# Another scheme of seven block products in a planned attention and feed-forward kernel

## The chip, the cores and the metric

The kernel runs on one core of a Trainium2 chip. The metric is the device time of one execution in microseconds; before the change the median of three runs is 946.24 us (943.14 to 946.65). The profile is of one more execution, which took 943.59 us, with 941.8 us from its first to its last instruction.

In the profile PE is TensorE (matmuls), PEld its loads of the stationary operand, DVE is VectorE, ACT is ScalarE, POOL is GpSimd, and SP issues DMAs. L441 is line 441 of the kernel. The clock column is the share of full speed that TensorE was granted.

## The reference

Two parts follow each other, all in float32:

```python
scores = scale * np.matmul(q, k.transpose(0, 1, 3, 2))        # 8 x 8 heads, 576 positions, 64 wide
mask = (rel >= 0) & (rel < 64)                                # each position sees itself and 63 before it
attn = softmax of the masked scores
attn_out = np.matmul(attn, v)
x = attn_out, tokens by heads                                 # 4608 x 512
h = x @ w_in                                                  # 512 x 2048
g = np.where(h >= 1, h, np.where(h <= -1, 0.0, (h + 1) ** 2 / 4.0))
out = g @ w_out                                               # 2048 x 512
```

## The kernel before, in words

**Tiles.** The 4608 tokens are nine tiles of 512. For each tile four attention steps `s` (128 tokens each, all heads) make the columns of x, and then the feed-forward part makes 16 blocks of 128 features from them and adds each block's share to four accumulators (L902).

**Two-part numbers.** Each operand of the feed-forward matmuls is split in a high part (rounded to TensorE's float32r) and a low part (the rest), and three matmuls stand for one: high-high, high-low, low-high. ACT or DVE rounds (copy and cast, L256 and L258), DVE or POOL subtracts (L527 for x, L885 for g, L716 for weights).

**An attention step.** Scores (L397) go to two PSUM banks, one for each half of the heads. From step 8 on, for each half apart: DVE scales and masks them into a tile `sm` (L409), finds the negative maximum (L413), ACT takes exponents and their sums (L420), DVE adds a small number and inverts (L427, L428), DVE or POOL normalises (L432), and DVE transposes 32-row pieces into a tile `ptd` (L441), 12 for each half. There are four tiles `sm` and three `ptd`. Then TensorE multiplies with v (L461). The result goes to a tile `u`.

**Seven products.** The first two tiles compute h plainly (L851). From the third tile on (`PLAIN = 2`), two feature blocks, two halves of the input features and two halves of the tile's tokens are a 2 x 2 by 2 x 2 block product that is done with seven products in place of eight (L786). The x side of the seven operands is made in a "build", one for each half of the columns of the tile: sums and differences of blocks (L511, L515), then the high and low parts `xs`. The weight side is made once, while the second tile runs (`sum_...`, L693, L704, L716), kept in HBM (`kept`) and loaded again for each tile in two rings (`wr`, tags `ra` and `rb`). A pair of feature blocks is computed by 24 matmuls (four products into two banks a and b, each of two halves of 256 columns), four dependent steps that empty these banks (L256 or L258, L802), then 18 matmuls (three products that add to what stands in the banks). The blocks of h stand in SBUF: the tile `h` has four blocks of 256 columns, two for each feature block. Before the change the first four products give two differences or sums of bank halves, the next three complete the two middle blocks in bank a (one copy of 512 columns), and SBUF blocks are added to each other (L806, L817, L818).

**The gate.** For each feature block: relu on ACT (L863), square (L868), min and max with h on DVE (L875), the high part `gh` on ACT (L880), the low part `gl` on POOL (L885), then 12 matmuls (L902). There are two buffers each of `a`, `gh` and `gl`.

**What sets the order.** The program adds items to a plan (`add`): a key (the place in the sequence at which the item is wanted), costs in ns for each engine that could do it, what it waits for, and which buffers it takes and gives back. `Plan.run` chooses again and again the item that can start first, within a patience the one of smallest key, puts it on its cheapest engine, and so writes each engine's instruction list. On the chip an engine works off its list in that order and waits where an operand is not ready.

Of the kernel before, what the change touches and what calls it, by code (L numbers as in the profile page):

```python
# [20 lines left out]
P = 128  # L21
# [61 lines left out]
BUFS = dict(qt=2, kt=2, vt=4, ps_a=2, sm=4, ptd=3, x=2, u=2, ps_h=2, a=2, gh=2, gl=2, acc=4, o=2, h=2, ra=2, rb=2, tmp=2)  # L83
# [5 lines left out]
B_KEY = 4 / 3  # L89
O_AFTER = 14 / 3  # L90
O_BEFORE = 0
EARLY_2 = 1.5
N_SPLIT = 8
# [6 lines left out]
A_EARLY = 1.5  # L100
# [85 lines left out]
def banded_attention_then_ffn(ctx: ExitStack, tc: tile.TileContext, q, k, v, w, masks, out, dims):  # L186
# [13 lines left out]
    att = ctx.enter_context(tc.tile_pool(name="att", bufs=BUFS["sm"]))  # L200
# [37 lines left out]
    ptd = [const.tile([P, NP, SB], F32, name=f"ptd{i}") for i in range(BUFS["ptd"])]  # L238
# [118 lines left out]

    def variant(s):
# [26 lines left out]
    def att_scores(s, masked, pool):  # L385
# [7 lines left out]
        for p in range(NP):  # L393
            for i in range(SB // m):
                r = slice(i * m, (i + 1) * m)
                for h in range(2):
# [3 lines left out]
                    )  # L400
        for h in range(2):
            blk[s, h] = banks[h][:, :, :n], att.tile([P, NP, WIN], F32, name="sm")[:, :, :n], *(
                att.tile([P, NP], F32, name=n) for n in ("nm", "den"))
# [30 lines left out]
    def att_transpose(s, h, i, js):  # L434


        sm, pt = blk[s, h][1], ptd[(2 * seq[s] + h) % len(ptd)]
        for j in js:
# [10 lines left out]
    def att_transposed(s, h, eng):  # L449
        copy(eng, ptd[(2 * seq[s] + h) % len(ptd)], pts.pop((s, h)))  # L450

    def att_values(s, pool):

        vt, pt = [vts.pop((s, i)) for i in range(2)], [ptd[(2 * seq[s] + h) % len(ptd)] for h in range(2)]
# [30 lines left out]
    def x_tiles(t):  # L485
# [9 lines left out]
        xops[t] = a, b, rest, [a[:, 0], rest[0], a[:, 1], b[:, 1], rest[1], rest[2], b[:, 0]]  # L495

    xtmp = {}

    def x_source(t, r, k):
        x = [xfs[t, r][:, j].rearrange("p (c e) n -> p e c n", e=2) for j in range(2)]  # L500
        if k == 0:
            return xtmp[t, r][:, :2]
        return (x[1], x[0][:, 0], x[1][:, 1], xtmp[t, r][:, 2])[k - 1]

    def x_sums(t, r, eng):
        xtmp[t, r] = d = ffn.tile([P, 4, 2, SB], F32, name="u", bufs=BUFS["u"])
        x = [xfs[t, r][:, j].rearrange("p (c e) n -> p e c n", e=2) for j in range(2)]
        for i, (a, b, op) in enumerate((
            (x[1][:, 0], x[1][:, 1], ALU.subtract), (x[0][:, 0], x[1][:, 1], ALU.add), (x[0][:, 1], x[0][:, 0], ALU.subtract)
        )):  # L510
# [600 lines left out]
```

## Time and profile before

| | |
|---|---|
| median of three runs | 946.24 us (943.14 to 946.65) |
| the profiled execution | 943.59 us, span 941.8 us |
| TensorE busy | 889.8 us, 94%, granted clock 0.979 |
| VectorE busy | 762.1 us, 81% |
| ScalarE busy | 523.7 us, 56% |
| GpSimd busy | 377.6 us, 40% |
| HBM | 162.15 MB read, 24.12 MB written, 198 GB/s over the span |

The shares are averages over stages: up to about 25 us q, k, v and weights arrive; to 250 us the two plain tiles run, the second with the weights' sums beside it; then seven tiles in cycles of about 100 us with four attention steps for the next tile in each; the last 80 us have no attention. A cycle is read best between two equal points, and a wait by what ended it.

### The profile page before, as it was taken

The page shows a single profiled execution, that of the slowest core. Times are in us where ns is not written, and L with a number is a line of the kernel's source. Part 1 is how long each engine was busy: PE and PEld are TensorE (multiplying, and loading weights), DVE is VectorE, ACT ScalarE, POOL GpSimd, SP SyncE. Part 2 cuts the span into 40 slices and gives each one's busy share as a digit, 9 for nine tenths or more (in the row PEclk, how much of TensorE's full clock was granted, in tenths as well). Part 3 has the DMA queues.
Part 4 walks back from the last instruction along what each step waited for, and adds up shares of the span by engine and source line. Part 5 has one row for each costly group of instructions (what it writes and reads, how often), then busy time and mean ns, then how long its engine had stood idle before and what let it go on. Part 6 is the DMA issues. An engine that isn't in the chain of part 4 may idle for free.

```text
span 941.8 us, 20899 instructions
## 1 busy us (share of the span) xinstructions
PE 889.8 (94%) x7839; PEld 766.9 (81%) x7839; DVE 762.1 (81%) x1800; ACT 523.7 (56%) x1322; POOL 377.6 (40%) x392
## 2 busy tenths in 40 slices
PE   7799998989789999899989999899989998999998
PEld 5688887867578888788878888788878887898997
DVE  6999997988999947979797989798887979774342
ACT  7898855555455545454554555445635554644443
POOL 1000035786453623436343545254433634352222
PEclk8999999999899999999999999999989999999999
DMA  8991148458376558476665667566846673647531
GB/s 322 402 355 46 57 137 280 155 198 278 120 243 234 179 180 270 138 235 208 212 214 186 213 189 242 180 209 205 254 134 211 205 258 113 190 158 220 178 118 45
DMA packets 108037, 187.63 MB, mean 199 GB/s; under 512 B 8480, under 2 KB 49696, under 8 KB 107936
## 3 DMA queue, kind: packets, MB, share of 16 engines
q1 hardware_dynamic: 107648, 185.38, 59.8%
q8 instruction: 62, 1.02, 0.4%
q10 hardware_dynamic: 288, 0.92, 0.3%
q14 instruction: 39, 0.32, 0.1%
HBM read 162.15 MB, written 24.12 MB: 198 GB/s over the span
## 4 chain that ended last, share of the span: by engine, by line
PE 51%; DVE 28%; ACT 6%; DMA 6%; issue 4%; POOL 4%; SPq 0%; ACTq 0%; DVEq 0%; POOLq 0%
PE acc L902 23%; PE ps_h L786 18%; DVE ptd L441 9%; PE ps_h L851 5%; DVE a L875 5%; ACT sm L420 3%; PE ps_a L461 2%; PE ps_a L397 2%; DMA kept<-half 2%; DVE u L511 2%; DMA kt<-in_k 2%; ACT a L863 1%; DVE xs L527 1%; DMA out<-o 1%; DVE sm L409 1%
## 5 line engine op out<-in xcount | busy, mean ns | idle before, releaser
L902 PE MATMUL acc<-wts,gh 128*128 128x512 f32 x1154 | 367.7, 400 | 18.5 <-ACT gh L880 15.9
L786 PE MATMUL ps_h<-xs,wr 128*128 128x256 f32 x2352 | 305.7, 285 | 2.5 <-DVE h L802 2.0
L786 PEld LDWEIGHTS ps_h<-xs,wr 128*128 128x128 f32 x2352 | 293.4, 192 | 15.4 <-DVE h L802 5.1
L885 POOL TENSOR_TENSOR gl<-a,gh 128x512 fp32r<-128x512 f32 (+1 forms) x130 | 172.0, 1324 | 316.8 <-ACT gh L880 273.9
L902 PEld LDWEIGHTS acc<-wts,gh 128*128 128x128 f32 x1154 | 213.7, 193 | 60.4 <-ACT gh L880 17.7
L902 PE MATMUL acc<-wts,gl 128*128 128x512 f32 x577 | 230.1, 399 | 7.8 <-POOL gl L885 7.5
L441 DVE STREAM_TRANSPOSE ptd<-sm 32x128 f32<-32x128 f32 x696 | 210.1, 302 | 11.1
L880 ACT CAST gh<-a 128x512 fp32r<-128x512 f32 (+1 forms) x149 | 89.5, 602 | 151.8 <-PE acc L902 95.5
L902 PEld LDWEIGHTS acc<-wts,gl 128*128 128x128 f32 x577 | 110.6, 192 | 37.4 <-POOL gl L885 13.5
L875 DVE SCALAR_TENSOR_TENSOR a<-a,h 128x512 f32<-128x512 f32 x112 | 96.2, 859 | 30.5 <-ACT a L868 28.8
L420 ACT ACTIVATE sm<-sm,nm 128x96 f32<-128x96 f32 (+1 forms) x256 | 93.2, 366 | 44.6 <-DVE nm L413 44.6
L863 ACT ACTIVATE a<-h 128x512 f32<-128x512 f32 x112 | 70.1, 626 | 64.1 <-DVE h L813 53.1
L851 PE MATMUL ps_h<-xh,wts 128*128 128x512 f32 (+1 forms) x296 | 87.8, 365 | 3.0 <-DVE a L875 1.9
L868 ACT ACTIVATE a<-a 128x512 f32<-128x512 f32 (+1 forms) x141 | 87.0, 617 | 4.3
L256 ACT COPY h<-ps_h 128x256 f32<-128x256 f32 (+1 forms) x102 | 46.7, 465 | 67.4 <-PE ps_h L786 67.0
L813 DVE TENSOR_TENSOR h<-h,ps_h 128x256 f32<-128x256 f32 x56 | 23.4, 419 | 69.3 <-PE ps_h L786 69.1
L693 POOL TENSOR_TENSOR half<-wts 128x256 f32<-128x256 f32 x18 | 13.4, 766 | 144.0 <-PE ps_h L851 127.0
L851 PEld LDWEIGHTS ps_h<-xh,wts 128*128 128x128 f32 x296 | 53.8, 190 | 12.5 <-DVE a L875 2.1
L802 DVE TENSOR_TENSOR h<-h,ps_h 128x256 f32<-128x256 f32 x112 | 46.7, 417 | 11.1 <-ACT h L256 8.3
L851 PE MATMUL ps_h<-xl,wts 128*128 128x512 f32 (+1 forms) x148 | 53.7, 363 | 0.5 <-DVE xl L474 0.5
L461 PEld LDWEIGHTS ps_a<-ptd,vt 128*64 128x64 f32 x992 | 33.4, 140 | 18.2 <-DVE ptd L441 6.6
L420 ACT ACTIVATION_READ_ACCUMULATOR sm<-sm,nm 128x1 f32 x256 | 48.2, 188 | 0.0
(101 smaller groups left out, 968.8 us busy)
## 6 DMA issues: line engine op xcount, KB each, us to landing
wr<-kept SPq DMA_DIRECT2D x112, 512.0 KB, 4.7
wr<-kept SPq DMA_DIRECT2D x112, 384.0 KB, 3.9
vt<-in_v SPq DMA_DIRECT2D x72, 256.0 KB, 4.0
kt<-in_k SPq DMA_DIRECT2D x35, 384.0 KB, 4.2
raw<-in_w SPq DMA_DIRECT2D x12, 1023.8 KB, 11.2
qt<-in_q SPq DMA_DIRECT2D x36, 256.0 KB, 3.6
out<-o SPq DMA_DIRECT2D x32, 256.0 KB, 4.3
kept<-wts SPq DMA_DIRECT2D x32, 128.0 KB, 2.1
```

What stands on the lines that cost most here:

```text
L256: nc.scalar.copy(dst, src)
L420: nc.scalar.activation(sm[:, p, :], (ps if masked else sm)[:, p, :], AF.Exp, bias=nm[:, p:p + 1], scale=scale if masked else 1.0, accum_ou ...
L441: nc.vector.transpose(pt[(c + j) * SQ:(c + j + 1) * SQ, :, r], sm[r, :, c * SQ:(c + 1) * SQ])
L461: nc.tensor.matmul(ps[half[h], p, n], lhsT=vt[i][:, c:c + D], rhs=pt[h][:, p, n], start=True, stop=True)
L786: nc.tensor.matmul(ps[:, c * 2 * SB:(c + 1) * 2 * SB], lhsT=r[:, part, cp, o], rhs=xo[k][:, xp, cp], start=i == 0 and c == 0 and j == 0 an ...
L851: nc.tensor.matmul(ps, lhsT=wts[f, 0][:, part, c * P:(c + 1) * P], rhs=x[:, c, r], start=(c == 0 and j == 0), stop=(c == NP - 1 and j == 2),)
L863: nc.scalar.activation(gs[t, f, r.start][0], phs[t, f, r.start], AF.Relu, bias=0.5, scale=0.5)
L868: nc.scalar.activation(a, a, AF.Square)
L875: nc.vector.scalar_tensor_tensor(out=a, in0=a, scalar=1.0, in1=ps, op0=ALU.min, op1=ALU.max)
L880: nc.scalar.copy(g[1], g[0])
L885: engine[eng].tensor_tensor(out=g[2], in0=g[0], in1=g[1].bitcast(F32), op=ALU.subtract)
L902: nc.tensor.matmul(acc[t, i][:, n], lhsT=g[:, sub], rhs=wts[f, 1][:, part, n], start=(q == 0 and j == 0), stop=(q == NF - 1 and j == 2 and ...
```

## The change

**Products.** Another scheme of seven products is used. Other sums of x and of weights are made: four differences of x blocks, each an item of its own (`x_sums`, before one item of three and a total), and four sums of weight blocks (before five), with three weight blocks copied unchanged instead of two. The four blocks of h are completed by adding from banks: one copy of 256 columns and three additions after the first 24 matmuls, two additions and a copy of 256 after the 18. No SBUF block is added to another.

**Halves of heads.** From step 8 on the two halves share one tile `sm` of double width (two such tiles), and one item each finds the maxima, inverts the sums, and transposes: 12 pieces of 32 x 256, each an item. They write the first two of the three `ptd` tiles, as one buffer (`pt2`).

**Order.** Costs of some items in the plan are larger, output matmuls of the first block of a tile and of the last are items of 128 tokens, and the keys of attention (`A_EARLY`) and of the outputs at the change from plain tiles (`O_CHANGE`) are other ones.

```diff
-BUFS = dict(qt=2, kt=2, vt=4, ps_a=2, sm=4, ptd=3, x=2, ...
+BUFS = dict(qt=2, kt=2, vt=4, ps_a=2, sm=2, ptd=3, pt2=1, x=2, ...
-A_EARLY = 1.5
+A_EARLY = 5
...
+    def att_transpose_both(s, i, j, c):
+        r = slice(i * QB + j * SQ, i * QB + (j + 1) * SQ)
+        src = blk[s, BOTH][1][r].rearrange("p h a n -> p (h a) n")
+        dst = ptq[(c + j) * SQ:(c + j + 1) * SQ, :2].rearrange("p h a n -> p (h a) n")
+        nc.vector.transpose(dst[:, :, r], src[:, :, c * SQ:(c + 1) * SQ])
...
+    def x_sums(t, r, j, eng):
+        if j == 0:
+            xtmp[t, r] = ffn.tile([P, 4, 2, SB], F32, name="u", bufs=BUFS["u"])
+        d = xtmp[t, r]
+        x0, x1 = x_halves(t, r)
+        i, a, b = ((0, x1[:, 0], x0[:, 0]), (2, x1[:, 1], x1[:, 0]), (1, x1[:, 1], d[:, 0]), (3, x0[:, 1], d[:, 1]))[j]
+        engine[eng].tensor_tensor(out=d[:, i], in0=a, in1=b, op=ALU.subtract)
...
-        return dict(DVE=65 * k + 1.04 * n, Pool=200 * k + 2.1 * n)
+        return dict(DVE=100 * k + 1.5 * n, Pool=200 * k + 2.3 * n)
...
+            (6, 2, 3, ALU.add), (4, 6, 0, ALU.subtract), (5, 0, 2, ALU.subtract), (7, 1, 4, ALU.subtract)
...
-            ((a, 0, 3, 0), (a, 1, 0, 1), (b, 0, 1, 2), (b, 1, 2, 3)),
-            ((a, 0, 2, 4), (a, 1, 0, 5), (b, 0, 1, 6)),
+            ((a, 0, 0, 0), (a, 1, 1, 1), (b, 0, 2, 2), (b, 1, 3, 3)),
+            ((b, 0, 2, 5), (b, 1, 0, 6), (a, 0, 1, 4)),
...
+    def h_copy(t, n, to, eng):
+        copy(eng, h_of(t, n)[:, to:to + 256], prods[t, n][0][:, :256])
+
+    def h_add(t, n, to, of, bank_, at):
+        h, ps = h_of(t, n), prods[t, n][bank_]
+        nc.vector.tensor_tensor(out=h[:, to:to + 256], in0=h[:, of:of + 256], in1=ps[:, at:at + 256], op=ALU.add)
...
+        m = [add(key, take, lambda e: h_copy(t, n, 512, e), [xa])]
+        for v in (256, 512, 0, 256), (768, 256, 1, 0), (768, 768, 1, 256):
+            m.append(add(key, cost, lambda e, v=v: h_add(t, n, *v), m[-1:]))
         xb = add(
             key + B_KEY, dict(PE=18 * (12.5 + 256 * .4175)), lambda e: ffn_products(t, n, 1), [rb, xa, *m],
...
+        xl = add(key, cost, lambda e: h_add(t, n, 512, 256, 1, 0), [xb, m[1]])
+        xf = add(key + Y_LATE, cost, lambda e: h_add(t, n, 256, 256, 1, 256), [xl], gives=[("ps_h", xa, 1)])
+        xm = add(key + Y_LATE, take, lambda e: h_copy(t, n, 0, e), [xb], gives=[("ps_h", xa, 0)])
...
-                ends = t == len(TILES) - 1 and q == NF - 1 and r.stop == TILES[t]
-                for i0 in subs(r) if ends else [None]:
+                by_sub = t >= PLAIN and q == 0 or t >= PLAIN - 1 and q == NF - 1
+                for i0 in subs(r) if by_sub else [None]:
```

**How it moves instructions.** Three places follow, first before, then with the change. The first is VectorE where it has most to do in a cycle. Before, that is the build of the first half of a tile (three sums, L511, stand just ahead); `ptd` and `sm` are attention's tiles, `xs` the operands, `h` the blocks of features, `a` the gate's tile.

```order
L441 STREAM_TRANSPOSE ptd_119<-sm 32x4x32 x3
L258 CAST xs<-u 128x2x128
L258 COPY h<-ps_h 128x512
L527 TENSOR_TENSOR xs<-u,xs 128x2x2x128
L813 TENSOR_TENSOR h<-h,ps_h 128x256
L527 TENSOR_TENSOR xs<-u,xs 128x2x128
L427 TENSOR_SCALAR den<-den 128x4
L428 RECIPROCAL den<-den 128x4
L527 TENSOR_TENSOR xs<-u,xs 128x2x128
L432 TENSOR_TENSOR sm<-sm,den 128x4x96
L441 STREAM_TRANSPOSE ptd_119<-sm 32x4x32 x3
L875 SCALAR_TENSOR_TENSOR a<-a,h 128x512
```

With the change the pair with most rows of VectorE's work is the one in which the build of the second half begins:

```order
L828 TENSOR_TENSOR h<-h,ps_h 128x256 x2
L447 STREAM_TRANSPOSE ptd<-sm 32x8x32
L828 TENSOR_TENSOR h<-h,ps_h 128x256
L447 STREAM_TRANSPOSE ptd<-sm 32x8x32 x10
L828 TENSOR_TENSOR h<-h,ps_h 128x256
L447 STREAM_TRANSPOSE ptd<-sm 32x8x32
L828 TENSOR_TENSOR h<-h,ps_h 128x256
L884 SCALAR_TENSOR_TENSOR a<-a,h 128x512 x2
L529 TENSOR_TENSOR u<-u 128x256 x4
L259 CAST xs<-u 128x2x2x128
```

The gates (L875, now L884) stood behind the build's sums and low parts, and now stand ahead of the sums; no low part of `xs` is in these rows any more.

The second place is VectorE in the other of the two builds of a tile, before the second half's:

```order
L802 TENSOR_TENSOR h<-h,ps_h 128x256
L258 COPY h<-ps_h 128x256
L802 TENSOR_TENSOR h<-h,ps_h 128x256
L806 TENSOR_TENSOR h<-h 128x256
L511 TENSOR_TENSOR u<-u 128x256 x3
L258 CAST xs<-u 128x2x128 x2
L258 COPY h<-ps_h 128x512
L813 TENSOR_TENSOR h<-h,ps_h 128x256
```

and with the change the first half's:

```order
L828 TENSOR_TENSOR h<-h,ps_h 128x256
L259 CAST xs<-u 128x2x2x128
L828 TENSOR_TENSOR h<-h,ps_h 128x256
L259 CAST xs<-u 128x2x128 x2
L828 TENSOR_TENSOR h<-h,ps_h 128x256
L418 SCALAR_TENSOR_TENSOR sm<-ps_a,nmsk 128x384 x2
L422 TENSOR_REDUCE nm<-sm 128x8
```

The build's casts stood behind the two additions that the 18 products wait for, and now three casts stand between the three additions (L828) that they wait for.

The third place is GpSimd's list around the build of the first half, before:

```order
L885 TENSOR_TENSOR gl<-a,gh 128x512
L527 TENSOR_TENSOR xs<-u,xs 128x2x128
L515 TENSOR_TENSOR u<-u 128x512
L817 TENSOR_TENSOR h<-h 128x256
L818 TENSOR_TENSOR h<-h 128x256
L527 TENSOR_TENSOR xs<-u,xs 128x2x2x128
L885 TENSOR_TENSOR gl<-a,gh 128x512 x2
```

and with the change:

```order
L894 TENSOR_TENSOR gl<-a,gh 128x512 x2
L529 TENSOR_TENSOR u<-u 128x256 x2
L894 TENSOR_TENSOR gl<-a,gh 128x512
L541 TENSOR_TENSOR xs<-u,xs 128x2x2x128 x2
L541 TENSOR_TENSOR xs<-u,xs 128x2x128 x3
L894 TENSOR_TENSOR gl<-a,gh 128x512 x2
```

All five low parts (L541) of this build are now GpSimd's, and the additions of blocks of `h` are gone from its list.

More of the change, by code (lines that the diff above doesn't have):

```diff
@@ L356, in banded_attention_then_ffn, with pt_of @@
     half = [slice(0, D), slice(D, P)]
+    def pt_of(s, h):
+        return h if s >= SOON else (2 * seq[s] + h) % len(ptd)
     def variant(s):
@@ L644, in add_step @@
-            ready.append(x)
+                    due, dict(DVE=440), lambda e, piece=piece: att_transpose_both(s, *piece),
+                    ready if ends else taken or x, takes=["pt2"] * (not n), gives=[("sm", xs)] * ends,
+                )
+                ready.append(x)
+                first = taken = taken or [x]
+            gives = [("pt2", taken[0])]
         last["t"] = first
         needs = ready + [xv, xw]
-        gives = [("ptd", taken[0]), ("ptd", taken[1]), ("vt", xv), ("vt", xw)]
+        gives += [("vt", xv), ("vt", xw)]
```

246 lines of the change are left out of this document (117 added, 129 removed).

## The prediction

> **What bounds the kernel now.** I read the page's busy times first, then stretches of the span, then what TensorE waited for, then one such wait in the timeline.
>
> ```profile
> PE 889.8 (94%) x7839; PEld 766.9 (81%) x7839; DVE 762.1 (81%) x1800; ACT 523.7 (56%) x1322; POOL 377.6 (40%) x392
> ```
>
> TensorE is nearly always busy and its instruction counts stay the same after the change (2352 products, 1731 output matmuls, all else equal), so only its waits and its clock can be won. Where are they? The next view is busy time by stretch (start:end, length, then busy us and instruction count of PE, PEld, DVE, ACT, POOL, then granted clock, DMA share, GB/s).
>
> ```profile
> 391.57:491.13 99.56, 95.31 (x913) 83.29 (x913) 85.38 (x209) 52.09 (x137) 45.34 (x43) 1.00 0.64 207
> 491.13:590.77 99.64, 96.31 (x912) 84.37 (x912) 85.37 (x209) 51.85 (x137) 45.37 (x43) 0.98 0.64 207
> 590.77:691.76 100.99, 96.38 (x913) 84.43 (x913) 85.38 (x209) 52.08 (x137) 45.34 (x43) 0.98 0.65 207
> 691.76:792.07 100.31, 97.47 (x912) 85.16 (x912) 85.36 (x209) 52.17 (x137) 45.28 (x43) 0.97 0.62 196
> 877.22:919.30 42.08, 42.08 (x267) 38.16 (x266) 17.04 (x36) 18.05 (x33) 10.54 (x8) 1.00 0.44 140
> 165.00:250.00 85.00, 75.21 (x664) 59.17 (x662) 76.79 (x188) 44.73 (x130) 63.24 (x77) 0.99 0.59 196
> 250.00:310.00 60.00, 54.35 (x566) 46.65 (x565) 57.02 (x144) 30.58 (x91) 23.44 (x24) 0.94 0.66 221
> ```
>
> The first four are whole cycles of a tile (eight pairs of feature blocks, four attention steps), on average 100.1 us. The fifth is four pairs of the last tile, with no attention beside them: 42.08 / 4 = 10.52 us each, with no gap. What a step adds to TensorE shows between two sets of 18 products:
>
> ```profile
> 605.15 2.32 PE L786 MATMUL ps_h<-xs,wr 128*128 128x256 f32 x18
> 610.14 0.99 PE L397 MATMUL ps_a<-kt,qt 64*32 64x96 f32 x64
> 616.79 2.32 PE L786 MATMUL ps_h<-xs,wr 128*128 128x256 f32 x18
> 627.40 1.15 PE L461 MATMUL ps_a<-ptd,vt 128*64 128x64 f32 x32
> 628.48 2.42 PE L786 MATMUL ps_h<-xs,wr 128*128 128x256 f32 x18
> ```
>
> 616.79 - 605.15 = 11.64 holds one set of scores, so scores cost 1.12; 628.48 - 616.79 = 11.69 holds one set of values, so values cost 1.17. A cycle that never waited would take 8 x 10.52 + 4 x 1.12 + 4 x 1.17 = 93.3 us. The four cycles are 6.8 us above that on average.
>
> ```profile
> PE acc L902 <- ACT gh L880: 15.9, 8, 4.7
> PE acc L902 <- POOL gl L885: 7.5, 9, 1.6
> PE ps_a L461 <- DVE ptd L441: 5.8, 6, 2.1
> ```
>
> The output matmuls (L902) wait for the gated activations gh and gl. One such wait closes each cycle; the timeline shows who is late:
>
> ```profile
> 687.27 1.29 POOL L527 TENSOR_TENSOR xs<-u,xs 128x512 fp32r<-128x512 f32 x1
> 687.46 1.38 DVE L527 TENSOR_TENSOR xs<-u,xs 128x256 fp32r<-128x256 f32 x1
> 688.03 0.63 ACT L868 ACTIVATE a<-a 128x512 f32<-128x512 f32 x1
> 689.34 0.94 DVE L441 STREAM_TRANSPOSE ptd<-sm 32x128 f32<-32x128 f32 x3
> 690.30 0.69 DVE L875 SCALAR_TENSOR_TENSOR a<-a,h 128x512 f32<-128x512 f32 x1
> 691.09 0.62 ACT L880 CAST gh<-a 128x512 fp32r<-128x512 f32 x1 [2.42 <-DVE a L875]
> 691.76 1.22 PE L902 MATMUL acc<-wts,gh 128*128 128x512 f32 x2 [2.76 <-ACT gh L880]
> 693.70 1.06 PE L902 MATMUL acc<-wts,gh 128*128 128x512 f32 x2
> ```
>
> ACT's cast waited for the gate on DVE (L875), and DVE had no gap: it was busy with the next tile's operands (L527), normalising and transposing. After the wait TensorE's pair of matmuls takes 1.06, a cost that the 6.8 includes. The pair of feature blocks in which it happens:
>
> ```profile
> 675.05:695.55 20.50, 17.16 (x114) 14.16 (x113) 19.38 (x42) 10.03 (x30) 10.86 (x10) 0.89 0.54 175
> ```
>
> From its first addition L802 to the next pair's, DVE has 19.38 us of work, against 11.7 (10.52 + 1.17) of TensorE's. So TensorE sets the pace over the cycle, and DVE, 85.4 of 100, sets it in one burst per cycle. Between 165 and 310 us (the weights' sums, the first products) DVE is busy 133.8 of 145 us; TensorE idles 9.8 + 5.65 = 15.4 us there, and the granted clock takes 85 x 0.01 + 60 x 0.06 = 4.5 more.
>
> **The change part by part.** Durations come from the groups by shape (count | busy us, mean ns of one | idle before):
>
> ```profile
> L441 DVE STREAM_TRANSPOSE ptd<-sm 32x128 f32<-32x128 f32 x696 | 210.1, 302 | 11.1
> L802 DVE TENSOR_TENSOR h<-h,ps_h 128x256 f32<-128x256 f32 x112 | 46.7, 417 | 11.1 <-ACT h L256 8.3
> L806 DVE TENSOR_TENSOR h<-h 128x256 f32<-128x256 f32 x27 | 17.9, 662 | 0.9
> L817 DVE TENSOR_TENSOR h<-h 128x256 f32<-128x256 f32 x31 | 15.7, 505 | 0.0
> L818 DVE TENSOR_TENSOR h<-h 128x256 f32<-128x256 f32 x31 | 15.3, 492 | 1.1
> L258 DVE COPY h<-ps_h 128x256 f32<-128x256 f32 x56 | 23.4, 417 | 5.6 <-PE ps_h L786 5.5
> L258 DVE COPY h<-ps_h 128x512 f32<-128x512 f32 x10 | 6.8, 678 | 0.0
> L527 DVE TENSOR_TENSOR xs<-u,xs 128x512 fp32r<-128x512 f32 x15 | 17.8, 1187 | 0.0
> L511 DVE TENSOR_TENSOR u<-u 128x256 f32<-128x256 f32 x36 | 19.7, 599 | 0.1
> L875 DVE SCALAR_TENSOR_TENSOR a<-a,h 128x512 f32<-128x512 f32 x112 | 96.2, 859 | 30.5 <-ACT a L868 28.8
> ```
>
> *Joined heads.* From step 8 on, 672 transposes of 32x128 become 336 of 32x256, which the trace does not hold. Below, one cannot take less than the narrow one (302); above, no more than two (604). The two copies of L258 give the slope: (678 - 417) / 256 = 1.02 ns an element, so 302 + 128 x 1.02 = 433 ns. I take 433, since that row is the same engine and width change. DVE loses 672 x 0.302 - 336 x 0.433 = 57 us (0 to 101).
>
> *The other seven products.* The SBUF additions L806, L817, L818 disappear: 17.9 + 15.7 + 15.3 = 48.9 us on DVE, and 79 more on POOL. Additions from banks go from 168 to 280: 112 x 0.417 = +46.7. Copies on DVE go from 56 narrow and 10 wide to 17 narrow: -16.3 - 6.8. Net -25 us. The four dependent steps ahead of the second products stay four, so that chain is no longer; behind the second products the even block now needs one copy beside two additions, where it needed a wide copy and two SBUF additions.
>
> *Smaller pieces.* The sums and differences of a build are separate items, so the planner puts 57 instead of 37 of the low parts L527 on POOL; DVE keeps 2 instead of 15 wide ones, 13 x 1.187 = -15 us.
>
> Together -97 us of DVE's 762, nearly all in seven tiles: 13.9 each, 85.4 down to 71.5 in 93.3. What decides is the burst. The fullest pair after the change (order above) has 5 x 0.417 + 12 x 0.433 + 2 x 0.859 + 4 x 0.599 = 11.4 us and one cast; TensorE's work there, with two sets of values, is 10.52 + 2.34 = 12.9. The gates stand ahead of the build's sums there, not behind.
>
> *The new wait.* The joined transposes write one buffer, so those of a step wait for the values of the step before. Queued behind on DVE is the third addition, for which the 18 products wait. The wait is at most one set of values, 1.15; TensorE has 12 output matmuls in between, 610.14 - 605.15 - 2.32 = 2.7, so it is covered. The next values come after 2.7 + 2.3 + 2.7 = 7.7 of TensorE's work; DVE's 12 transposes and two additions take 6.0 (covered by 1.7) or, at 604 ns, 8.1 (0.4 late).
>
> *The casts among the additions.* In the build of the first half of a tile, three casts now stand between the four steps that the 18 products wait for, and they wait for two sums on POOL. Two such casts in the trace, one beside a POOL instruction:
>
> ```profile
> 683.18 1.29 POOL L515 TENSOR_TENSOR u<-u 128x512 f32<-128x512 f32 x1
> 683.36 1.26 DVE L258 CAST xs<-u 128x256 fp32r<-128x256 f32 x1
> 273.12 0.26 DVE L258 CAST xs<-u 128x256 fp32r<-128x256 f32 x1
> ```
>
> So they add 0.8 to 3.8 us to a chain of 4 x 0.417 = 1.7; TensorE covers 2.7 + 1.12 = 3.8 with outputs and scores. Late by nothing to 1.7, and POOL's sums can add one or two. I let a cycle keep 2.0 of its 6.8 us, with ends of 0 and 4.
>
> *The rest.* Split output items, two double tiles sm in place of four and three copies of weight blocks in place of two issue the same matmuls and the same number of DMAs (506 on SP), off the waits above: I cost them at nothing; they would cost if the queue of weight loads were late, and no wait of TensorE's names it.
>
> *Sum.* Five such waits close cycles (391, 491, 590, 691 and 792 us): 5 x (6.8 - 2.0) = 24. Of the 19.9 us between 165 and 310 I take half, 10 (ends 0 and 19.9): of DVE's work ahead of the first product the transposes alone lose 147 x 0.302 - 24 x 0.302 - 60 x 0.433 = 11 us, but the weights' sums still pass through POOL, ACT and DMA. The profiled execution took 943.59 us (span 941.8): 943.6 - 24 - 10 = 909.6. That execution lies 2.7 under the median shown, near the fastest of its three; I leave the forecast at 910.
>
> **The rivals.** *The burst moves instead of going* (the casts, one transpose buffer): each cycle keeps 4 of 6.8 and the front gives 5: 943.6 - 14 - 5 = 925. For it: the chain with casts has no cover to spare. Against: every pair's DVE work is at or under TensorE's.
>
> *Nothing changes*: the gate's own steps, not DVE's queue, end the wait; with two buffers for gh and gl no lighter DVE helps, 942. Against: the gate began at 690.30, 1.6 us after its square had ended (688.66), with DVE busy throughout.
>
> *Slower*: POOL, with 20 more of the low parts, holds DVE up as in the row at 683.36. A tile's two builds have about 6.4 casts and low parts on DVE; at 1.0 late each (1.26 - 0.26), all in the chain of additions, and 2 us of half-speed matmuls behind, that is 8.4 a cycle against 6.8 now: over six tiles +10, nothing won in front, 953. It decides once a cycle's lateness passes 6.8. Against: POOL loses 79 additions, and additions from banks stood at 417 throughout. The Trainium skill, page "SBUF — State Buffer", section "SBUF: two separate sides", states this as a lock on a port pair that VectorE and GpSimd share, held for a whole instruction by whichever began first. By that rule these casts do wait in full; the rows at 683 agree (1.26 beside 1.29), and the additions that the change takes out were of the kind it names.
>
> **How the numbers follow.** Forecast 0.65 (896 to 922), moved burst 0.22, no change 0.07, slower 0.06. The ends of the terms give 943.6 - 34 - 19.9 = 890 and 943.6 - 14 - 0 = 930; 896 to 930 holds 8 in 10. A measurement here can tell about 0.5%, 4.7 us: faster 0.88, same 0.06, slower 0.06.
>
> **What would show it.** Right: 336 wide transposes near 433 ns; DVE near 72 of a cycle of 95 us; output matmuls without waits of 2 us at a cycle's end; granted clock 1.00 in every cycle. Wrong: the wide transpose near 604; products (the 18) waiting for additions, with casts of 1 us or more between them; values waiting for transposes; TensorE idle 15 us between 165 and 310 as before.

## The result, and the profile after

The changed kernel takes 920.5 us (median of four runs, 918.86 to 921.3) beside 946.44 of the kernel before in the same comparison: a ratio of 0.9729, 95% interval 0.9702 to 0.9757, faster by 2.7%. The forecast was 910 with a range of 896 to 930. The profiled execution took 920.28 us, its span 918.5; beside the profiled execution before (943.59), from which the forecast took off 34 us, that is 23.3 (26 by the medians). Medians below are of four executions each; with narrow transposes on other partitions one execution took 4790 us, and the median is that of the other three.

Busy times on the page:

```profile
PE 879.8 (96%) x7839; PEld 762.4 (83%) x7839; DVE 667.5 (73%) x1348; ACT 503.5 (55%) x1297; POOL 317.7 (35%) x305
```

VectorE lost 762.1 - 667.5 = 94.6 us, where 97 were forecast. The span fell by 23.3: TensorE's busy time by 10.0 (the granted clock rose from 0.979 to 0.987), its idle time by 13.3. Groups by shape (count | busy us, mean ns of one | idle before):

```profile
L447 DVE STREAM_TRANSPOSE ptd<-sm 32x256 f32<-32x256 f32 x336 | 146.3, 435 | 8.0 <-POOL sm L441 2.2
L259 DVE CAST xs<-u 128x256 fp32r<-128x256 f32 x19 | 20.1, 1082 | 0.0
L541 POOL TENSOR_TENSOR xs<-u,xs 128x512 fp32r<-128x512 f32 x26 | 34.3, 1330 | 23.7 <-DVE xs L259 22.0 <-DMA wr<-kept 1.1 <-ACT xs L257 0.6
L541 POOL TENSOR_TENSOR xs<-u,xs 128x256 fp32r<-128x256 f32 x31 | 26.0, 861 | 0.0
```

The wide transpose takes 435 ns, and 57 low parts are on GpSimd. One row is out of line: a cast of 128x256, 568 ns on average before, now takes 1082. Stretches (start:end, length, then busy us and count of PE, PEld, DVE, ACT, POOL, granted clock, DMA share, GB/s); the first four are cycles, the last two the front:

```profile
365.69:462.13 96.44, 94.02 (x913) 83.02 (x913) 72.39 (x146) 49.48 (x136) 36.58 (x32) 1.00 0.65 211
462.13:557.50 95.37, 94.05 (x913) 83.06 (x913) 71.32 (x146) 49.28 (x136) 35.12 (x31) 1.00 0.65 211
557.50:653.92 96.42, 94.04 (x912) 83.04 (x912) 72.36 (x146) 49.87 (x137) 37.89 (x33) 1.00 0.66 220
653.92:750.32 96.40, 94.02 (x912) 83.03 (x912) 72.37 (x146) 49.58 (x136) 36.56 (x32) 1.00 0.65 215
165.00:244.00 79.00, 74.48 (x592) 59.05 (x592) 72.14 (x133) 39.52 (x107) 52.42 (x62) 0.96 0.51 173
244.00:310.00 66.00, 61.33 (x627) 54.53 (x622) 48.46 (x104) 34.19 (x98) 25.53 (x22) 0.95 0.66 218
```

A cycle is 96.2 us on average: 3.9 less than before, and 2.9 above the 93.3 of a cycle without waits. Of the 3.9, TensorE's busy time gives 2.3 (96.4 to 94.0 on average; the granted clock was 0.97 to 1.00 before and is 1.00 now) and its idle time 1.6. In the front TensorE still idles 4.5 + 4.7 = 9.2 us, and the clock takes 79 x 0.04 + 66 x 0.05 = 6.5. The waits say on what:

```profile
PE ps_h L812 <- DVE h L828: 14.0, 10, 3.5
PE ps_h L860 <- DVE a L884: 7.8, 3, 3.7
```

No output matmul waits for 2 us at a cycle's end any more, and in a cycle no values wait for transposes. Instead the 18 products (L812) wait for the additions (L828): once 3.54 us at 277.53, then at the cycles' ends (1.9 us in four of five, 0.85 at 557.50). The timeline at 462 us shows who holds the addition up:

```profile
453.26 3.04 PE L812 MATMUL ps_h<-xs,wr 128*128 128x256 f32 x24
455.17 1.71 POOL L894 TENSOR_TENSOR gl<-a,gh 128x512 fp32r<-128x512 f32 x1
455.75 1.67 DVE L884 SCALAR_TENSOR_TENSOR a<-a,h 128x512 f32<-128x512 f32 x1
457.35 0.87 DVE L529 TENSOR_TENSOR u<-u 128x256 f32<-128x256 f32 x2
458.14 0.41 DVE L828 TENSOR_TENSOR h<-h,ps_h 128x256 f32<-128x256 f32 x1
458.47 0.42 DVE L259 CAST xs<-u 128x512 fp32r<-128x512 f32 x1
458.80 0.42 DVE L828 TENSOR_TENSOR h<-h,ps_h 128x256 f32<-128x256 f32 x1
459.03 4.70 POOL L541 TENSOR_TENSOR xs<-u,xs 128x512 fp32r<-128x512 f32 x5 [2.16 <-DVE xs L259]
459.13 2.62 DVE L259 CAST xs<-u 128x256 fp32r<-128x256 f32 x2
461.67 0.41 DVE L828 TENSOR_TENSOR h<-h,ps_h 128x256 f32<-128x256 f32 x1
462.13 1.09 PE L812 MATMUL ps_h<-xs,wr 128*128 128x256 f32 x7 [1.92 <-DVE h L828]
```

The 24 products end at 456.30. VectorE begins the first addition 1.84 us later, after a gate that took 1.67 beside a GpSimd instruction (0.69 where nothing is beside it) and two sums of the build. Then two casts, 0.26 us each where nothing is beside them, take 2.62 beside GpSimd's run of low parts, and the last addition stands behind them. Matmuls run at half speed behind some waits only:

```profile
277.53:282.00 4.47, 4.47 (x20) 4.37 (x21) 4.00 (x10) 0.22 (x1) 0.40 (x1) 0.50 0.36 142
462.13:466.00 3.87, 3.87 (x38) 3.34 (x46) 2.91 (x6) 1.97 (x9) 2.85 (x4) 1.00 0.89 301
```

The granted clock was 0.50 behind the wait at 277 and behind that at 195 us, and 1.00 behind those at 366, 462, 558 and 654.

### The profile page after: what moved, and what is told of

The parts are those of the page before. It is cut to its first block, busy times and chain, and to the rows that moved or that the text cites. A ratio compares the mean times of both kernels' runs of the same rounds, so it can differ in the third digit from the quotient of the medians.

```text
span 918.5 us, 20359 instructions
## 1 busy us (share of the span) xinstructions
PE 879.8 (96%) x7839; PEld 762.4 (83%) x7839; DVE 667.5 (73%) x1348; ACT 503.5 (55%) x1297; POOL 317.7 (35%) x305
## 4 chain that ended last, share of the span: by engine, by line
PE 64%; DVE 21%; ACT 6%; DMA 4%; issue 3%; POOL 2%; SPq 0%; ACTq 0%; DVEq 0%
PE acc L911 30%; PE ps_h L812 22%; DVE ptd L447 6%; PE ps_h L860 6%; DVE a L884 3%; PE ps_a L476 2%; PE ps_a L401 2%; DVE h L828 2%; ACT a L872 2%; ACT sm L429 2%; DVE xs L259 2%; DVE half L733 2%; DVE u L529 2%; DMA kt<-in_k 2%; DMA kept<-half 1%
## 5 line engine op out<-in xcount | busy, mean ns | idle before, releaser
L911 PE MATMUL acc<-wts,gh 128*128 128x512 f32 x1154 | 363.0, 396 | 0.2 <-ACT o L257 0.2
L812 PEld LDWEIGHTS ps_h<-xs,wr 128*128 128x128 f32 x2352 | 296.1, 191 | 26.4 <-DVE h L828 18.2
L812 PE MATMUL ps_h<-xs,wr 128*128 128x256 f32 x2352 | 304.3, 285 | 14.0 <-DVE h L828 14.0
L911 PEld LDWEIGHTS acc<-wts,gh 128*128 128x128 f32 x1154 | 208.3, 189 | 41.2 <-ACT o L257 0.6
L911 PE MATMUL acc<-wts,gl 128*128 128x512 f32 x577 | 225.2, 390 | 0.3 <-POOL gl L894 0.3
L828 DVE TENSOR_TENSOR h<-h,ps_h 128x256 f32<-128x256 f32 x280 | 116.7, 417 | 109.7 <-PE ps_h L812 80.8
L447 DVE STREAM_TRANSPOSE ptd<-sm 32x256 f32<-32x256 f32 x336 | 146.3, 435 | 8.0 <-POOL sm L441 2.2
L884 DVE SCALAR_TENSOR_TENSOR a<-a,h 128x512 f32<-128x512 f32 x112 | 86.5, 772 | 57.9 <-ACT a L877 56.9
L860 PE MATMUL ps_h<-xh,wts 128*128 128x512 f32 (+1 forms) x296 | 91.9, 379 | 10.1 <-DVE a L884 7.8
L257 ACT COPY h<-ps_h 128x256 f32<-128x256 f32 x95 | 35.3, 371 | 118.5 <-PE ps_h L812 118.2
L877 ACT ACTIVATE a<-a 128x512 f32<-128x512 f32 (+1 forms) x140 | 86.3, 617 | 4.4
L541 POOL TENSOR_TENSOR xs<-u,xs 128x256 fp32r<-128x256 f32 (+1 forms) x57 | 60.0, 1075 | 23.7 <-DVE xs L259 22.0
L724 POOL TENSOR_TENSOR half<-wts 128x256 f32<-128x256 f32 x18 | 13.5, 769 | 132.7 <-PE ps_h L860 126.6
L441 POOL TENSOR_TENSOR sm<-sm,den 128x384 f32<-128x384 f32 x30 | 32.3, 1082 | 66.3 <-DVE den L437 62.2
```

Of the source, the lines that this page charges most:

```text
L447: nc.vector.transpose(dst[:, :, r], src[:, :, c * SQ:(c + 1) * SQ])
L541: engine[eng].tensor_tensor(out=x_target(t, r, k, 1), in0=x_source(t, r, k), in1=x_target(t, r, k, 0).bitcast(F32), op=ALU.subtract)
L812: nc.tensor.matmul(ps[:, c * 2 * SB:(c + 1) * 2 * SB], lhsT=r[:, part, cp, o], rhs=xo[k][:, xp, cp], start=i == 0 and c == 0 and j == 0 an ...
L828: nc.vector.tensor_tensor(out=h[:, to:to + 256], in0=h[:, of:of + 256], in1=ps[:, at:at + 256], op=ALU.add)
L860: nc.tensor.matmul(ps, lhsT=wts[f, 0][:, part, c * P:(c + 1) * P], rhs=x[:, c, r], start=(c == 0 and j == 0), stop=(c == NP - 1 and j == 2),)
L877: nc.scalar.activation(a, a, AF.Square)
```

## The experiments

The theory to test had three parts: the gain comes from VectorE's work getting out of the way of what TensorE waits for; what is left of a cycle's excess is the casts that wait beside GpSimd; and the front (up to the first cycle) follows the same rule. The rivals are in each expectation.

The kernels order their matmuls differently, so a time at which one of them reaches "the first product" is not comparable: the changed kernel has 1908 matmuls behind it there, the one before 1996. I therefore use *lateness*: the start of a matmul minus what all matmuls ahead of it cost without a wait (from the rows of the prediction: 10.5 us a pair, 1.12 a set of scores, 1.17 a set of values; for other shapes the code's own 12.5 ns + 0.4175 ns a column). This work sums to 859.8 us in every run. "Front" is the lateness after 320 us of work, just ahead of the first wait that closes a cycle; "after it" is what the rest adds up to the last matmul.

| run | median us | ratio to before (95%) | VectorE busy | front | after it |
|---|---|---|---|---|---|
| before | 946 | | 762.1 | 44.6 | 33.4 |
| changed | 920.5 | 0.9729 (0.9702 to 0.9757) | 667.5 | 38.4 | 16.4 |
| narrow transposes, same partitions | 930.6 | 0.9829 (0.9800 to 0.9857) | 689.2 | 38.8 | 24.8 |
| narrow transposes, other partitions | 959.0 | 1.0160 (1.0130 to 1.0191) | 729.1 | 47.8 | 45.8 |
| old scheme of products | 935.1 | 0.9873 (0.9847 to 0.9898) | 726.1 | 49.4 | 19.2 |
| larger items | 951.5 | 1.0080 (1.0054 to 1.0106) | 683.8 | 45.3 | 40.2 |
| attention at the old keys | 921.6 | 0.9756 (0.9727 to 0.9785) | 644.7 | 39.1 | 17.9 |
| casts on ScalarE, order kept | 908.5 | 0.9591 (0.9563 to 0.9618) | 650.4 | 39.2 | 3.2 |
| low parts swapped | 914.3 | 0.9663 (0.9645 to 0.9681) | 663.7 | 38.0 | 11.3 |
| casts on ScalarE, order anew | 911.1 | 0.9631 (0.9612 to 0.9651) | 664.6 | 36.8 | 9.6 |
| mixed order | 910.8 | 0.9649 (0.9621 to 0.9677) | 641.0 | 36.0 | 10.0 |
| low parts on VectorE | 920.7 | 0.9726 (0.9698 to 0.9754) | 690.4 | 37.3 | 18.0 |
| sums of weights cut | 916.0 | 0.9693 (0.9673 to 0.9714) | 641.0 | 40.6 | 9.8 |
| before, casts on ScalarE | 939.3 | 0.9926 (0.9909 to 0.9944) | 752.9 | 47.3 | 26.3 |

Each ratio is to runs of the kernel before in the same comparison. By lateness the change won 6.2 us in the front and 17.0 after it, together 23.2 of the 23.3 that the spans differ by.

### What remains of a cycle: the casts

```diff
-        copy(eng, x_target(t, r, k, 0), x_source(t, r, k))
+        copy("ACT", x_target(t, r, k, 0), x_source(t, r, k))
```

> The changed kernel, with the 32 casts of operands that VectorE makes given to ScalarE, everything else in the same order. Theory A (a cast between the additions waits for GpSimd's running instruction, 2.62 us for two that take 0.26 each alone, and closes each cycle with a wait of 1.9 us): the wait at 365, 462, 557, 653 and 750 us falls under 0.5, the cycles from 96.2 to 94.5 or less, the time to 907 to 913 us. Rival B (the additions are late for another reason, or ScalarE, which gets 13 us more, is late in its turn): within 3 us of 920.5.

Measured: 908.5 us, and the cycles, from the sixteenth pair's start on, in the same columns as above:

```profile
440.82:534.34 93.52, 93.52 (x914) 83.21 (x913) 68.37 (x141) 51.70 (x142) 36.43 (x31) 1.00 0.66 220
628.73:722.24 93.51, 93.51 (x913) 83.22 (x912) 68.37 (x141) 51.54 (x142) 36.57 (x31) 1.00 0.66 220
```

In these two TensorE no longer waits at all: 93.52 of 93.52 us busy, the 93.3 of the prediction's floor; the cycle between them holds one wait of 0.63. ScalarE took the 13 us (503.5 to 516.2 busy) without being late. But this run takes the casts out of VectorE's queue altogether. Was it their waiting, or their place? The next run leaves them there and lets them begin first. The low parts are emitted when their five casts are, the last one first (only the first two change places):

```diff
-        engine[eng].tensor_tensor(out=x_target(t, r, k, 1), ...
+        todo = wait.setdefault((t, r), [])
+        todo.append((k, eng))
+        if len(cast[t, r]) == 5 or k == 1:
+            while todo:
+                x_low_now(t, r, *todo.pop())
```

> The changed kernel; only the first two low parts of each half-tile's operands change places, so that GpSimd's run of low parts begins after ScalarE's cast and not after VectorE's first one, some 0.7 us later; the casts stay on VectorE, where they stand. Theory A (VectorE's casts wait for whatever GpSimd instruction has begun; begun first, they take 0.26 each): the pair of casts that takes 2.62 us falls under 0.8, the wait of 1.9 us at the end of the cycles goes, 908 to 914 us, near the kernel with the casts on ScalarE (908.5). Rival B (the casts cost by their place in VectorE's queue or by ScalarE's part in the chain): within 3 us of 920.5.

Measured: 914.3 us, 0.3 above theory A's range and 3 below rival B's. The same place in this kernel's timeline (its lines are shifted by 10 from L541 on), and the group of its casts:

```profile
456.75 0.41 DVE L838 TENSOR_TENSOR h<-h,ps_h 128x256 f32<-128x256 f32 x1
457.08 0.49 DVE L259 CAST xs<-u 128x256 fp32r<-128x256 f32 x2
457.48 0.41 DVE L838 TENSOR_TENSOR h<-h,ps_h 128x256 f32<-128x256 f32 x1
...
457.76 4.62 POOL L551 TENSOR_TENSOR xs<-u,xs 128x512 fp32r<-128x512 f32 x5 [2.95 <-ACT xs L257]
...
457.99 2.37 PE L822 MATMUL ps_h<-xs,wr 128*128 128x256 f32 x18
```

```profile
L259 DVE CAST xs<-u 128x256 fp32r<-128x256 f32 x19 | 9.0, 501 | 0.0
```

The two casts take 0.49 where they took 2.62, on the same engine, in the same place, because GpSimd's run begins 0.7 us after them; the products follow without a wait. Two of five cycles still close with a wait of 1.89 (at 649 and 746 us), the others with 0.4 to 0.9 one pair later, so it wins 6 us and not 12. Those two are the better proof. There ScalarE's cast came 0.8 us earlier against VectorE's list, and GpSimd began ahead of the same casts:

```profile
645.97 4.68 POOL L551 TENSOR_TENSOR xs<-u,xs 128x512 fp32r<-128x512 f32 x5 [2.13 <-ACT xs L257]
646.10 2.58 DVE L259 CAST xs<-u 128x256 fp32r<-128x256 f32 x2
535.56:629.86 94.30, 93.86 (x914) 83.06 (x912) 70.30 (x146) 49.59 (x137) 36.80 (x31) 1.00 0.67 219
629.86:727.06 97.20, 95.31 (x914) 84.50 (x912) 71.98 (x146) 49.92 (x137) 36.44 (x31) 0.98 0.64 212
```

One execution of one kernel, the same stretch of VectorE's list: a cycle of 94.3 us where the casts began first, of 97.2 where GpSimd did. It is the waiting beside GpSimd that costs, then, not the place. The Trainium skill, page "SBUF — State Buffer", section "SBUF: two separate sides", says that the pair of ports that VectorE and GpSimd share goes, for a whole instruction, to whichever began first; among VectorE's instructions that need it the section has those with two inputs in SBUF (against a GpSimd instruction that reads SBUF) and fp32 copies from SBUF to SBUF. The rows agree: 0.49 or 2.58 to 2.62 for the casts by who began, 0.41 to 0.42 throughout for the additions, which have one input in a bank.

Did casts close the cycles before the change, too?

> The kernel before the change, with the 26 casts of operands that VectorE makes (13.4 us) given to ScalarE, the order otherwise the same. Theory A (before the change a burst of all of VectorE's work closes the cycle, casts are a small part of it): 937 to 944 us, the cycles stay above 98 us. Rival B (the casts beside GpSimd's instructions were the cause before, too): 920 to 930 us, the cycles fall to 95 or less.

The edit is the first one of this section, in the kernel before. Measured: 939.3 us, and a cycle of it:

```profile
447.68:546.12 98.44, 95.13 (x914) 83.35 (x913) 83.95 (x205) 53.74 (x142) 44.93 (x44) 1.00 0.66 209
```

That is 0.7% by the ratio, and 98.3 us a cycle beside 100.1: 1.8 less, where the same edit after the change took 96.2 to 93.8. Five of the 6.8 us stay without any cast of operands on VectorE, so before the change they were not what closed most of a cycle.

Next, does the gain hang on one order? Here the plan is told that casts go to ScalarE alone and arranges everything anew:

```diff
-        return dict(ACT=90 + .84 * n, DVE=65 + 1.05 * n)
+        return dict(ACT=90 + .84 * n)
```

> The changed kernel with the casts of operands allowed on ScalarE alone, and the order made anew (in the kernel with casts on ScalarE it was kept). If the gain is the casts' own it stays: 904 to 913 us. If it hung on the one order, the time goes back to 917 to 924 us.

Measured: 911.1 us. It does not hang on it. The front is better by 2 us, the cycles worse by 6; taking this order for the operands of the first two tiles only (`t <= PLAIN + 1`), and the other for the rest:

> The kernel with all casts of operands on ScalarE; the order is made anew with that in mind for the operands of the first two tiles that use products (where that order had the smaller lateness), and as in the changed kernel for the later ones. If the front of the one and the cycles of the other go together: 903 to 907 us. If the order of the front sets how the cycles fall: 908 to 914 us.

Measured: 910.8 us, the second outcome. The lowest median of this study remains that of the casts on ScalarE with the order kept, 908.5 us, 1.4% under the changed kernel with intervals that don't meet.

GpSimd's side of the lock can be emptied instead:

```diff
-            x = add(due, tt(n), lambda e, k=k: x_low(t, r, k, e), ...
+            x = add(due, dict(DVE=100 + 1.5 * n), lambda e, k=k: x_low(t, r, k, e), ...
```

> The changed kernel, with the low parts of the operands (57 of them on GpSimd, 60 us) allowed on VectorE alone; the order is made anew. Theory A (what counts is GpSimd's instructions beside VectorE's): a cast of 128x256 falls from 1.08 to under 0.4 us, the gate from 772 to under 740 ns, the wait that closes a cycle falls under 0.5, 908 to 916 us. Rival B (what counts is VectorE's load, which grows by 57 low parts of 0.4 to 1.2 us): the wait stays or grows, 923 to 935 us.

Measured: 920.7 us, neither outcome. The casts do what theory A says:

```profile
L259 DVE CAST xs<-u 128x256 fp32r<-128x256 f32 x7 | 2.5, 375 | 0.0
```

The gate fell to 747 ns, not under 740. What TensorE waits for moved:

```profile
PE ps_h L860 <- DVE a L884: 12.1, 5, 5.7
```

Products wait for additions 3.1 us in all, where it was 14.0. But VectorE has 690.4 us of work, and the plain products wait 12.1 us for the gate, where it was 7.8 (one wait, 5.7 us at 240, stands behind nine transposes); outputs wait 4.1 us for gl, values 3.4 for transposes. Relief and load came out even; this run separates nothing by itself.

### What the joined heads are worth

```diff
-        nc.vector.transpose(dst[:, :, r], src[:, :, c * SQ:(c + 1) * SQ])
+        for h in range(2):
+            m = slice(h * NP, (h + 1) * NP)
+            nc.vector.transpose(dst[:, m, r], src[:, m, c * SQ:(c + 1) * SQ])
```

> The changed kernel, with each 32x256 transpose issued as two of 32x128 behind each other; the order on every engine is otherwise the same. VectorE gets 336 x (2 x 0.302 - 0.435) = +57 us, 8 in each cycle of a tile. Theory A (VectorE's bursts set the pace, so the joined heads carry more than half of the gain): 928 to 936 us, the cycles of 96.2 us grow by 1 to 2.5. Rival B (the transposes lie beside TensorE's work and the other parts carry the gain): within 3 us of 920.5.

Measured: 930.6 us, inside theory A's range, though 10 of the 26 us is not the half of the gain that it names. And VectorE got 21 us more, not 57:

```profile
L449 DVE STREAM_TRANSPOSE ptd<-sm 32x128 f32<-32x128 f32 x672 | 167.0, 281 | 6.5 <-POOL sm L441 0.8
```

672 x 0.281 is 189 us, yet their busy time together is 167: the second of two transposes on the same partitions starts 235 ns after the first and overlaps it. So the same was tried with two pieces at a time, first one half of the heads of both, then the other (`m // 6, m // 3 % 2, m % 3` are a piece's indices):

```diff
+        for m in (n // 2 * 2, n // 2 * 2 + 1):
+            att_transpose_one(s, n % 2, m // 6, m // 3 % 2, m % 3)
```

> The changed kernel with its 336 transposes of 32x256 issued as 672 of 32x128, as in the run with narrow transposes, but ordered so that two in a row never write the same partitions (there, two on the same partitions started 235 ns apart and VectorE got only 21 us more; in the kernel before they start 317 ns apart). VectorE gets 672 x 0.302 - 146 = +57 us. Theory A (time follows VectorE's load in the cycles: 10 us of time came with those 21): 938 to 948 us, that is, the joined heads alone are worth the whole gain. Rival B (a cycle has room for some of it, and only what falls between the additions counts): 928 to 935 us.

Measured: 959.0 us, above both outcomes, and slower than before the change. Its transposes, a cycle, and what TensorE waits for (lines shifted by 5):

```profile
L452 DVE STREAM_TRANSPOSE ptd<-sm 32x128 f32<-32x128 f32 x672 | 203.1, 302 | 10.2
```

```profile
457.20:559.94 102.74, 96.78 (x913) 85.00 (x912) 81.42 (x194) 49.66 (x137) 36.88 (x31) 0.98 0.61 200
```

```profile
PE ps_h L817 <- DVE h L833: 24.5, 16, 3.9
PE ps_a L481 <- DVE ptd L452: 10.7, 16, 1.1
```

A cycle has VectorE busy 81.4 of 102.7 us. With VectorE's work in a cycle going from 72 us to 75.7 (the run above) a cycle grew from 96.1 to 98.7, and to 102.4 with 81.2 (the same three cycles in each): 0.7 us of time for each us of VectorE's work, though that engine has a fifth of the cycle free. The values wait for transposes, too, 0.8 us twice in a cycle, where the prediction put 0.4 for transposes of 604 ns into the one buffer. The order here was made for transposes of 440 ns and kept, so 959.0 tells what they cost in this order, not in the best one for them.

### What the scheme of products is worth

Here the product scheme, its sums and the additions behind it are those before the change; the rest (joined heads, keys, pieces of transposes and outputs) is the changed kernel's:

```diff
-            ((a, 0, 0, 0), (a, 1, 1, 1), (b, 0, 2, 2), (b, 1, 3, 3)),
-            ((b, 0, 2, 5), (b, 1, 0, 6), (a, 0, 1, 4)),
+            ((a, 0, 3, 0), (a, 1, 0, 1), (b, 0, 1, 2), (b, 1, 2, 3)),
+            ((a, 0, 2, 4), (a, 1, 0, 5), (b, 0, 1, 6)),
...
-    def h_add(t, n, to, of, bank_, at):
+    def h_first(t, n, i, eng):
```

> The changed kernel with the old scheme of seven products (its sums of weights and of operands, its additions on SBUF, its order of the operands); joined heads, output pieces and keys as after the change. VectorE gets back some 25 us by the prediction's terms, and the four sums of a build are one item again. Theory A (gain in proportion to VectorE's load: 25 to 40 of 97): 925 to 932 us. Rival B (the scheme of products is worth nothing by itself): within 3 us of 920.5. Rival C (the SBUF additions, which take turns with GpSimd's, were the larger part): 935 us and more.

Measured: 935.1 us, the lower edge of rival C, with 59 us more of VectorE's work where the prediction's terms said 25. By its rows the additions and copies of `h` make 23 of the 59. Another 16.5 are low parts: the order was made anew, and 18 of them came back from GpSimd. The build's sums are larger items again, too, so the run does not isolate the scheme, and rival C's reason is not shown. Where the time lies is in the table: 11.0 of its 13.8 us of lateness are in the front, 2.8 after it. The longest waits there are 4.1 us for gl at 216 us and 3.9 for additions at 261. In the cycles the new scheme is worth little by this.

### What the smaller pieces are worth

The same instructions, in larger items:

```diff
-        for j in range(1, 4):
-            xs = add(due, tt(2 * SB), lambda e, j=j: x_sums(t, r, j, e), [xs])
+        xs = i0 = add(due, tt(8 * SB, 4), lambda e: [x_sums(t, r, j, e) for j in range(4)], ...
...
-            for n, piece in enumerate(pieces_):
+            for n in range(2):
-                    due, dict(DVE=440), lambda e, piece=piece: att_transpose_both(s, *piece),
+                    due, dict(DVE=6 * 440), lambda e, n=n: [att_transpose_both(s, *p) for p in pieces_[6 * n:6 * n + 6]],
```

> The changed kernel with larger items in the order: the four sums of a half-tile's operands as one item, the twelve transposes of a step as two items of six; same instructions, order made anew. Theory A (small items let the additions through, and GpSimd take more low parts): 926 to 934 us. Rival B (where the items are cut doesn't matter once VectorE's work is small enough): within 3 us of 920.5.

Measured: 951.5 us, 17 above the upper end of theory A. VectorE is busy 683.8 us, 72% of the span, no more than in the changed kernel by share. Of its 16.3 us more, 11.8 are casts of operands that take longer (37.4 in place of 25.6); the 9 low parts that came back from GpSimd are only 3.6. The timeline of one wait shows what stands in the way (lines shifted by 3):

```profile
501.42 0.41 DVE L825 TENSOR_TENSOR h<-h,ps_h 128x256 f32<-128x256 f32 x1
501.75 5.38 DVE L447 STREAM_TRANSPOSE ptd<-sm 32x256 f32<-32x256 f32 x12
507.16 0.88 DVE L825 TENSOR_TENSOR h<-h,ps_h 128x256 f32<-128x256 f32 x2
...
508.09 1.22 PE L809 MATMUL ps_h<-xs,wr 128*128 128x256 f32 x4 [2.86 <-DVE h L825]
```

The 18 products had ended at 504.3 (501.89 + 2.42); the two additions behind them came after twelve transposes without a break, and the next pair's products waited 2.86 us for the banks. In the changed kernel additions stand between the transposes. How the 31 us divide between the transposes, the sums and the order that was made anew around them stays open.

### The front

The gate at 195 us is late by a normalisation and two sums of weights that run beside GpSimd's low parts. Its square (L877) had ended at 192.16. These are rows of the changed kernel's timeline:

```profile
186.85 0.76 DVE L724 TENSOR_TENSOR half<-wts 128x256 f32<-128x256 f32 x2
...
191.24 4.04 POOL L541 TENSOR_TENSOR xs<-u,xs 128x512 fp32r<-128x512 f32 x4
191.35 1.62 DVE L441 TENSOR_TENSOR sm<-sm,den 128x384 f32<-128x384 f32 x1
192.90 1.80 DVE L724 TENSOR_TENSOR half<-wts 128x256 f32<-128x256 f32 x2
194.62 0.68 DVE L884 SCALAR_TENSOR_TENSOR a<-a,ps_h 128x512 f32<-128x512 f32 x1
...
195.35 0.79 PE L860 MATMUL ps_h<-xh,wts 128*128 128x512 f32 x1 [3.68 <-DVE a L884]
```

The casts are not to blame there: with all of them on ScalarE the waits at 195 and 277 us were 4.04 and 4.56. On top of that edit, the two instructions of L724 and the four of L733 were made items of their own:

```diff
-            x = add(k, tt(4 * P, 4), lambda e, c=c: sum_sums(n, c, e), [x0])
+            for i in range(4):
+                x = add(k, tt(P), lambda e, c=c, i=i: sum_sums(n, c, e, i), [x])
```

> The changed kernel with all casts of operands on ScalarE (order kept) and the sums of weights cut into pieces of one instruction, as the change did with the sums of operands; the order is made anew around them. Theory A (in the front the gate at 195 us waits for whole items of sums ahead of it): the wait of 4.0 us at 195 us falls under 2, lateness ahead of the first product falls by 2 to 4, 903 to 907 us. Rival B (what stretches them is GpSimd's low parts beside them, in whatever pieces): within 3 us of 908.5 or worse.

Measured: 916.0 us against 908.5. The wait at 191 us fell to 1.42 as expected, but the order made anew put a gate behind ten transposes (lines shifted by 4):

```profile
234.30 4.48 DVE L447 STREAM_TRANSPOSE ptd<-sm 32x256 f32<-32x256 f32 x10
238.81 0.69 DVE L888 SCALAR_TENSOR_TENSOR a<-a,ps_h 128x512 f32<-128x512 f32 x1
...
239.56 0.80 PE L864 MATMUL ps_h<-xh,wts 128*128 128x512 f32 x1 [5.78 <-DVE a L888]
```

One wait went and a longer one came: small items alone don't decide what stands ahead of what, and the front's lateness grew by 1.4 us where 2 to 4 less were expected. No run here isolates what keeps the front late. And the keys of attention, a part of the order that the prediction gave no term:

```diff
-A_EARLY = 5
+A_EARLY = 1.5
```

> The changed kernel with the attention steps of a tile scheduled 1.5 ahead of its products, as before the change, in place of 5; order made anew, same instructions. Theory A (the earlier start is what lets TensorE do more between the first products and gives the operands their time): 926 to 936 us. Rival B (it moves work, not waits): within 3 us of 920.5.

Measured: 921.6 us, no difference that can be told from the changed kernel (intervals 0.9727 to 0.9785 and 0.9702 to 0.9757), in time as rival B has it. But waits did move: the 1.9 us at the cycles' ends are gone, and once a cycle the values wait 2.38 us for VectorE's scaling of scores (L418). The equal time comes of two different waits, so it is a coincidence and not a sign that the keys do nothing.

Of the theory's three parts the second is shown: the casts were moved in two ways, and within one execution. The first is borne out where more transposes stood in a kept order. The third is argued from rows alone.

## Why the prediction was right, and where it was off

**What bounds.** Right: TensorE paces, VectorE's work in the way of it makes the waits, and the matmuls didn't change. The waits of outputs for gh and gl are gone from the cycles' ends, and the granted clock is 1.00 in each cycle; of the 3.9 us that a cycle won, 2.3 are TensorE's busy time. One of the signs that the prediction named for being wrong showed all the same: the 18 products wait for additions, with casts of over 1 us between them.

**VectorE's work.** Right in sum, 97 forecast and 94.6 measured; the wide transpose 433 and 435 ns, a cycle's load 71.5 and 72. The rows before and after bear out two of the terms: transposes lose 56.5 (57 forecast), products 25.3 (25). Low parts lose 20 (15 forecast). That the rest comes to so little is in part luck: casts of operands take 12 us more, normalisations 9 and sums of weights 6, the gate 10 less and the inverses 11 less, none of which the sum has.

**What a cycle keeps: 2.0 of 6.8 us.** The mechanism was named (casts between the additions, beside GpSimd) and is shown by two runs; the size was 2.9. The bound "late by nothing to 1.7" was passed by a little: 1.92. The casts are not the reason: the three take 3.04 us together, inside the 0.8 to 3.8 allowed, and TensorE covers 3.9 (3.8 forecast). The chain was taken to begin when the products end; it began 1.84 us later, behind the gate and two sums, a term put at nothing. With the keep of 2.0, five cycles would have won 24; the cycles shown won 3.9 each, and the lateness behind the front fell by 17.0.

**The front: half of 19.9.** Mis-sized, and this is the larger relative miss: 6.2 us of lateness went, not 10. (In the prediction's own window, 165 to 310 us, idle time and clock take 15.7 of the 19.9 us still, but other work stands in it.) Two waits stayed, 3.68 at 195 us and 3.54 at 277, each with half-speed matmuls behind; lateness grows by 7.0 and 6.4 in the 20 us of work around them. By the rows VectorE's sums, gates and normalisations there run beside GpSimd's low parts (0.76 or 1.80 for the same two sums); that this is the cause is argued from the rows, not shown by a run. I had put the same rows' port rule among the rivals for the cycles and not applied it to the front. The transposes were not the whole story: giving all of their work back costs 9.4 there, the old products 11.0.

**Smaller pieces.** Priced as 15 us of VectorE's load, with split items at no cost or gain of their own. The load was near (20 us by the rows), but it is not what the pieces are worth: larger items put 3.6 us of low parts back and cost 31 us of time, in an order made anew around them.

**The rivals.** *Burst moves*: in part true. Its 925 lies 4.5 us from 920.5, the forecast's 910 lies 10.5: in the cycles the forecast was nearer (2.9 stayed, where the forecast kept 2.0 and the rival 4), in the front the rival (6.2 won, where it gave 5 and the forecast 10). *Slower by the shared port*: the lock was there, but cost 1.9 us once a cycle and not 8.4, since it stretched two casts that stood ahead of an addition, not six, and the matmuls behind them kept their speed in four of five cycles. *Nothing changes*: refuted, the gate's own steps did not hold.

The parts don't add: undone one at a time they cost 15 (products), 31 (pieces) and 10 to 39 us (transposes), and together they bring 26. Each was undone inside an order that had been arranged around the others.

## What to carry to other kernels

An engine at 72% can pace another one: ask what stands ahead of the instruction that the pacing engine waits for, and cut long runs of work at that place before counting busy time. A short copy or sum in SBUF on VectorE can wait out a GpSimd instruction that began first (here casts of 0.26 us took 1.3, sums of 0.4 took 0.9), so let it begin first, or give it to ScalarE. And compare kernels with another order at equal work done, not at equal names in the program.

## What was not expected of the hardware

Two narrow transposes (32x128) that write the same partitions start 235 ns apart and overlap by some 65 ns; on other partitions they start 317 apart, at 302 each. So 672 of them take 167 or 203 us of VectorE's time by their order alone. The wide one, 435 ns, starts 448 ns after the one ahead of it.

Two waits of the changed kernel are alike, 1.92 us at 462 and at 750 us, for the same addition. The granted clock behind the first was 1.00, behind the second 0.59 (750.32 to 754.50). No run here shows why.
